# Block-sparse attention and a SoLU layer: a new order of the PV matmuls, full-row mask matmuls and an earlier fill of V's ones, in a kernel whose order of work is planned at build time

## The chip, the cores and the metric

The kernel runs on one core of one Trainium2 chip. The metric is the device time of one execution in microseconds. Executions come in a fast state and, some of them, in a slower one; only fast ones are compared here. Most slow executions here take 4 to 5 us longer. Profiles of three of them (pv_alone, pv_up_half, estimate) were kept: matmuls with 128 columns start 107 ns apart until 16.3 to 17.2 us and 56 ns apart later, while in the fast profile of the kernel before this change of pace comes at 4.7 us. The granted clock of the page (0.988 to 1.0 in these three) does not show it.

## The reference

Inputs are q, k, v of shape (4, 8, 768, 64), a list of three sampled key blocks for each of 24 query blocks, and the weights of a feed-forward layer.

```python
def _attn_ref(q, k, v, sampled_blocks):
    ...
    scores = scale * np.matmul(q, k.transpose(0, 1, 3, 2))
    mask = np.abs(blk_i - blk_j) <= 1                      # neighbouring blocks of 32
    mask = mask | (blk_i == 0) | (blk_j == 0) | (blk_i == n_blocks - 1) | (blk_j == n_blocks - 1)
    ...                                                    # and the sampled blocks
    scores = np.where(mask, scores, -1000000000.0)
    attn = softmax(scores)
    return np.matmul(attn, v)

def _moe_ref(x, w_in, w_out, g_ln):                        # x: (3072, 512)
    h = x @ w_in                                           # (3072, 1024)
    solu = h * softmax(h)
    ln = (solu - mean) / np.sqrt(var + 1e-06) * g_ln
    return (ln @ w_out).astype(np.float32)
```

## The kernel before

The mask is part of the score product: 24 further rows hold, on K's side, a one-hot code of the key block and, on Q's side, that query block's row of penalties. A score matmul therefore has 64 + 24 = 88 rows. For each batch, pair of heads and 256 queries there are three score steps of four matmuls, one exponential each on ScalarE, and three PV steps of eight matmuls:

```python
            def pv(o, n=n, pv0=pv0):
                acc = bank(pv0 or o)[:, 0 : 4 * (D + 1)].rearrange("p (a h d) -> p a h d", a=2, h=2)
                for m in range(4):
                    hh, jc = divmod(4 * n + m, NCH)
                    for qt in range(2):
                        nc.tensor.matmul(acc[:, qt, hh, :],
                                         exb[exs[n].slot][:, m, qt * P : (qt + 1) * P],
                                         va[i][:, 2 * pr + hh, jc, :], start=(n + m + qt == 0),
                                         stop=(n == 2 and m == 3 and qt == 1), skip_group_check=True)
```

V has a 65th column of ones, so that the softmax's sums come with the product.

The kernel describes its work as some 1,270 operations, each with an engine, an estimated time, its dependencies, the buffers that it takes from small pools, and a number `due`, its priority. A list scheduler inside the kernel walks through them at build time, and the instructions are then written out in exactly the order that it found:

```python
                    late = t > now + 0.02
                    key = (t if late else now, o.due)
                    if best is None or key < best[0]:
                        best = (key, o, max(t, now))
...
    A = [-275.62, -525.80, -272.33, -662.68, -957.45, -272.29, -386.71, -239.28, -1009.88, -78.24, -51.10,
...
    F = [-470.15, -35.44, -36.49, 309.28, 479.54, 383.62, -287.11, 438.46, 358.81, 675.40, 541.54, 632.99,
...
    Q = [-607.56, -1401.48, -624.25, -553.21, -198.33, 1231.82, 1169.17, 552.20, -1665.24, 7.66, 761.23,
```

`A`, `F` and `Q` are the priorities of the attention units, the feed-forward tiles and the preparations of Q and K. They look like what they are: numbers found by a search. The layer's gain g gets into w_out. A small matmul `gt` turns g, in one of two PSUM banks ("m") that it shares with the PV steps and the transposes; then VectorE scales the eight parts of w_out, which until then lie in buffers that batch 1's K and Q need:

```python
    gt = op("PE", 0.1, lambda o: nc.tensor.matmul(bank(o)[:, 0:KF], g8, identf[0:KF, 0:KF], start=True, stop=True),
            [g_load, idf, stage[("k", 0, 2)]], due=15, take="m")
    gc = op("DVE", 0.1, lambda o: nc.vector.tensor_copy(out=g_sb, in_=bank(gt)[:, 0:KF]), [gt], due=15,
            last_of=[gt])
...
    wo = [op("DVE", 0.39, lambda o, c=c: nc.vector.tensor_scalar(
        out=w_out_sb[:, c, :], in0=w_out_f[c], scalar1=g_sb[:, c : c + 1], scalar2=None,
        op0=ALU.mult), [w_out_load[c // 3], gc], due=26) for c in range(KF)]
```

The softmax here doesn't subtract the row's maximum and nothing guards it: scores larger than these inputs give would overflow.

## Time and profile before

| | before |
|---|---|
| median of 3 runs | 207.44 us (207.4 to 208.06) |
| profiled span | 205.7 us, granted clock 1.0 |
| TensorE busy | 197.6 us (96%) |
| ScalarE busy | 173.9 us (85%) |
| VectorE busy | 152.6 us (74%) |

In a profile's line of a group, `x576 | 85.4, 272 | 0.5` reads: 576 instructions, 85.4 us busy, 272 ns for one, 0.5 us of idle time before them. A matmul's own duration overlaps with that of the next (a PV matmul is recorded with 193 ns, while they start 31 ns apart), so costs are taken from the distance of two starts. A line of busy time by stretch has the stretch, its length, then PE (matmuls), PEld (weight loads), DVE (VectorE), ACT (ScalarE) and POOL (GpSimd), each with its number of instructions, then the granted clock, the DMA engines' share and GB/s.

### The profile page before, as it was taken

The page shows a single profiled execution, that of the slowest core. Times are in us where ns is not written, and L with a number is a line of the kernel's source. Part 1 is how long each engine was busy: PE and PEld are TensorE (multiplying, and loading weights), DVE is VectorE, ACT ScalarE, POOL GpSimd, SP SyncE. Part 2 cuts the span into 40 slices and gives each one's busy share as a digit, 9 for nine tenths or more (in the row PEclk, how much of TensorE's full clock was granted, in tenths as well). Part 3 has the DMA queues.
Part 4 walks back from the last instruction along what each step waited for, and adds up shares of the span by engine and source line. Part 5 has one row for each costly group of instructions (what it writes and reads, how often), then busy time and mean ns, then how long its engine had stood idle before and what let it go on. Part 6 is the DMA issues. An engine that isn't in the chain of part 4 may idle for free.

```text
span 205.7 us, 5857 instructions
## 1 busy us (share of the span) xinstructions
PE 197.6 (96%) x2304; PEld 143.1 (70%) x2332; DVE 152.6 (74%) x361; ACT 173.9 (85%) x215; POOL 63.7 (31%) x131
## 2 busy tenths in 40 slices
PE   7899999999999999999999999999999999999993
PEld 6599988777777778667777777776777655454442
DVE  4997889996788796864848675679887658788720
ACT  6799999999999999889999999998998928456532
POOL 5134015436542252154321244153310111224220
PEclk9999999999999999999999999999999999999999
DMA  5999999699996988489998969799642954668462
GB/s 155 353 381 367 261 309 116 194 270 265 307 191 155 301 211 135 87 300 246 180 232 202 247 178 195 156 328 245 118 104 66 133 163 57 150 141 189 133 205 102
DMA packets 71375, 41.80 MB, mean 203 GB/s; under 512 B 54316, under 2 KB 66868, under 8 KB 71348
## 3 DMA queue, kind: packets, MB, share of 16 engines
q1 hardware_dynamic: 70752, 40.38, 80.3%
q0 software_dynamic: 544, 1.05, 2.7%
q8 instruction: 18, 0.29, 0.6%
q14 instruction: 9, 0.07, 0.1%
q10 hardware_dynamic: 52, 0.00, 0.0%
HBM read 23.07 MB, written 6.29 MB: 143 GB/s over the span
## 4 chain that ended last, share of the span: by engine, by line
PE 85%; DVE 5%; ACT 4%; issue 2%; DMA 1%; POOL 1%; DVEq 0%; ACTq 0%; POOLq 0%
PE sbank L504 28%; PE mbank L636 20%; PE sbank L580 18%; PE mbank L525 14%; ACT ex L515 3%; DVE w_out_sb L402 3%; PE mbank L467 2%; DMA samp_i<-in_sampled_blocks_dram 1%; PE sbank L703 1%; DVE ot L647 1%; PE mbank L555 1%; ACT eso L589 1%; PE sbank L467 1%; DVE kb L445 1%; DVE x L539 0%
## 5 line engine op out<-in xcount | busy, mean ns | idle before, releaser
L515 ACT ACTIVATE ex<-sbank 128x1024 bf16<-128x1024 f32 x144 | 138.4, 1032 | 8.9 <-PE sbank L504 7.6
L504 PE MATMUL sbank<-qT,kT 88*128 88x256 bf16 x576 | 85.4, 272 | 0.5
L504 PEld LDWEIGHTS <-kT 88*128 88x128 bf16 x576 | 52.2, 97 | 23.0 <-issue 2.1
L580 PE MATMUL sbank<-w_in_sb,xT 128*128 128x512 bf16 x174 | 48.5, 379 | 0.7
L525 PEld LDWEIGHTS <-ex 128*128 128x128 bf16 x1152 | 45.0, 97 | 4.7 <-DVE x L539 0.2
L636 PE MATMUL mbank<-w_out_sb,eso 128*128 128x512 bf16 (+1 forms) x190 | 46.5, 370 | 1.0 <-DVE ot L647 0.5
L525 PE MATMUL mbank<-va,ex 128*128 128x65 bf16 x1152 | 47.2, 193 | 0.0
L593 DVE SCALAR_TENSOR_TENSOR eso<-sbank,eso 128x1024 bf16<-128x1024 f32 x24 | 29.3, 1220 | 12.1 <-ACT eso L589 12.1
L589 ACT ACTIVATE eso<-sbank 128x1024 bf16<-128x1024 f32 x24 | 24.8, 1035 | 12.0 <-PE sbank L580 4.6
L636 PEld LDWEIGHTS <-eso 128*128 128x128 bf16 x200 | 18.8, 98 | 15.5 <-issue 0.6
L606 DVE BATCH_NORM_STATS2 bn<-eso 128x6 f32<-128x512 bf16 x40 | 25.6, 682 | 0.2
L580 PEld LDWEIGHTS <-xT 128*128 128x128 bf16 x192 | 17.9, 98 | 10.3
L613 POOL TENSOR_SCALAR mv<-se,mv 128x1 f32<-128x1 f32 x24 | 6.9, 287 | 55.4 <-DVE mv L609 44.5
L647 DVE TENSOR_SCALAR ot<-mbank,rs 128x512 f32<-128x512 f32 (+1 forms) x19 | 13.9, 734 | 11.6 <-PE mbank L636 6.0
L536 DVE RECIPROCAL r<-mbank 128x4 f32<-128x4 f32 x48 | 8.4, 176 | 17.9 <-PE mbank L525 17.6
L539 DVE TENSOR_TENSOR x<-mbank,r 128x256 bf16<-128x256 f32 x48 | 19.9, 418 | 0.7
L486 POOL CAST va<-vst 128x768 bf16<-128x768 f32 x16 | 14.1, 881 | 17.2 <-DMA vst<-in_v_dram 17.1
L421 POOL CAST kb<-kst 128x768 bf16<-128x768 f32 x12 | 10.0, 831 | 21.3 <-DMA kst<-in_k_dram 21.2
L617 POOL TENSOR_TENSOR rs<-mv,neg_half 128x1 f32<-128x1 f32 x24 | 14.4, 602 | 6.6 <-ACT ot L650 3.5
L421 POOL CAST qb<-qst 128x768 bf16<-128x768 f32 x12 | 10.3, 861 | 13.1 <-DMA qst<-in_q_dram 8.6
L597 DVE TENSOR_SCALAR eso<-eso,mu 128x1024 bf16<-128x1024 bf16 x24 | 12.5, 523 | 0.2
L611 POOL TENSOR_TENSOR se<-se 128x1 f32<-128x1 f32 x24 | 4.9, 203 | 19.3 <-ACT eso L589 19.1
(74 smaller groups left out, 115.0 us busy)
## 6 DMA issues: line engine op xcount, KB each, us to landing
vst<-in_v_dram SPq DMA_DIRECT2D x16, 384.0 KB, 5.1
out_dram<-ot SPq DMA_DIRECT2D x23, 256.0 KB, 2.5
kst<-in_k_dram SPq DMA_DIRECT2D x15, 384.0 KB, 5.5
qst<-in_q_dram SPq DMA_DIRECT2D x15, 384.0 KB, 5.2
w_in_sb<-in_moe_w_in_dram POOLq DMA_DIRECT2D x2, 512.0 KB, 11.3
kT<-in_moe_w_out_dram SPq DMA_DIRECT2D x1, 768.0 KB
qT<-in_moe_w_out_dram SPq DMA_DIRECT2D x1, 768.0 KB, 13.0
eso<-in_moe_w_out_dram SPq DMA_DIRECT2D x1, 512.0 KB
```

What stands on the lines that cost most here:

```text
L421: nc.gpsimd.tensor_copy(out=half(cb[o.slot], 0).rearrange("p (c h d) -> p c h d", c=NCH, h=2), in_=st[ld.slot].rearrange("p h c d -> p c h ...
L504: nc.tensor.matmul(s[:, m, :], kT[i][0:DM, pr, hh, jc * P : (jc + 1) * P], qT[i][0:DM, pr, hh, t * TW : (t + 1) * TW], start=(m % 2 == 0), ...
L515: exs.append(op("ACT", act_us(1024), lambda o, so=so: nc.scalar.activation(out=exb[o.slot], in_=sbank[so.slot], func=ACT.Exp, scale=scale) ...
L525: nc.tensor.matmul(acc[:, qt, hh, :], exb[exs[n].slot][:, m, qt * P : (qt + 1) * P], va[i][:, 2 * pr + hh, jc, :], start=(n + m + qt == 0) ...
L539: nrm = op("DVE", 0.41, lambda o: nc.vector.tensor_tensor(out=xb[x_of[(b, t)].slot][:, :, 2 * pr * D : (2 * pr + 2) * D].rearrange("p a (h ...
L580: nc.tensor.matmul(h[:, f * 512 : (f + 1) * 512], xTb[xp.slot][:, a, c, :], w_in_sb[:, c, f * 512 : (f + 1) * 512], start=(c == 0), stop=( ...
L589: se = op("ACT", act_us(d_ff) + 0.22, lambda o, h0=h0: nc.scalar.activation(out=eb[o.slots["e"]], in_=pair(h0), func=ACT.Exp, accum_out=se ...
L593: so = op("DVE", 1.3, lambda o, h0=h0, se=se: nc.vector.scalar_tensor_tensor(out=sob[o.slot], in0=pair(h0), scalar=1.0, in1=eb[se.slots["e ...
L606: bn = op("DVE", 2 * 0.68, lambda o, so=so: [nc.vector.bn_stats(out=bnb[o.slot][:, f], in_=sob[so.slot][:, f * 512 : (f + 1) * 512]) for f ...
L617: rs = op("POOL", 0.55, lambda o, mv=mv: nc.gpsimd.tensor_tensor(out=rsb[o.slot], in0=mvb[mv.slot][:, 0:1], in1=neg_half, op=ALU.pow), [q2 ...
L636: nc.tensor.matmul(bank(o0 or o)[:, 0:w], sotb[st.slot][:, f, :], w_out_sb[:, f, col : col + w], start=(f == 0), stop=(f == KF - 1))
L647: nc.vector.tensor_scalar(out=otb[o.slot][:, 0:w], in0=bank(o0)[:, 0:w], scalar1=rsb[rs.slot], scalar2=None, op0=ALU.mult)
```

## The change

The intent: PV matmuls in an order that streams better; mask matmuls that use all 128 rows (zeros past the 24) and so need no change of the array's mode; V's ones by VectorE while it has nothing to do; the mask earlier at the start. Cut to its core:

```diff
+    PV_ORDER = [(3 - m, a) for a in range(2) for m in range(4)]
...
-    w0 = op("DVE", 0.1, lambda o: nc.vector.memset(warm, 0.0), due=-100)
+    w0 = op("DVE", 0.1, lambda o: nc.vector.memset(warm, 0.0), due=-2199.5)
...
-    selq = const.tile([NB, NCH, P], BF16, name="selq")
+    selq = const.tile([P, NCH, P], BF16, name="selq")
...
-    maskq = const.tile([NB, NB], BF16, name="maskq")
+    maskq = const.tile([P, NB], BF16, name="maskq")
...
+    sqz, mqz = fill(selq, 0.0, -2195.9), fill(maskq, 0.0, -2195.8)
...
+    for kr in krow:
+        plan.follow(kr, mq)
...
-        for lo, hi, due in ((0, TW, -2088), (TW, S, -2084.6))]
+        for lo, hi, due in ((0, TW, -2101), (TW, S, -2084.6))]
...
-    vones = [op("POOL", 0.3, lambda o, i=i: nc.gpsimd.memset(va[i][:, :, :, D : D + 1], 1.0), [stat],
-                due=-1900 if i == 0 else 0) for i in range(2)]
+    vones = [op("DVE", 0.15, lambda o, i=i: nc.vector.memset(va[i][:, :, :, D : D + 1], 1.0), due=-2195 + i)
+             for i in range(2)]
...                                          # w_in loaded by halves of its columns
-                            plan.follow(f, cas[0])
+                            plan.follow(f, qrow[(0, 0)])
...
-                for m in range(4):
+                for k, (m, qt) in enumerate(PV_ORDER):
                     hh, jc = divmod(4 * n + m, NCH)
-                    for qt in range(2):
...                                          # the matmul itself is the same; filler counts rounded otherwise;
                                           # the mask's estimate for the planner is 0.2, not 0.24
```

More of the change, by code (lines that the diff above doesn't have):

```diff
@@ L336 @@
             [last, io, samp_dma], due=-2089)
-    mq = op("DVE", 0.24, lambda o: nc.vector.scalar_tensor_tensor(
-        out=maskq, in0=anyeq, scalar=1.0, in1=static, op0=ALU.subtract, op1=ALU.mult), [last, stat], due=-2088)
+    mq = op("DVE", 0.2, lambda o: nc.vector.scalar_tensor_tensor(
+        out=maskq[0:NB], in0=anyeq, scalar=1.0, in1=static, op0=ALU.subtract, op1=ALU.mult), [last, stat, mqz], due=-2088)
     def selq_tr(o):
@@ L345 @@
     sqt = op("PE", NCH * 0.056, selq_tr, [ohs, mids], due=-2190, take="m")
-    sqs = op("ACT", 0.75, lambda o: nc.scalar.copy(out=flat(selq), in_=bank(sqt, BF16)[0:NB, 0:S]), [sqt],
+    sqs = op("ACT", 0.75, lambda o: nc.scalar.copy(out=flat(selq)[0:NB], in_=bank(sqt, BF16)[0:NB, 0:S]), [sqt, sqz],
              due=-2189, last_of=[sqt])
-    krow = [op("DVE", 0.36, lambda o, hh=hh: nc.vector.tensor_copy(out=kT[0][D:DM, 0, hh, :], in_=flat(selq)), [sqs],
+    krow = [op("DVE", 0.36, lambda o, hh=hh: nc.vector.tensor_copy(out=kT[0][D:DM, 0, hh, :], in_=flat(selq)[0:NB]), [sqs],
                due=(-2087.5, -2079.8)[hh]) for hh in range(2)]
+    for kr in krow:
+        plan.follow(kr, mq)
     mps = lambda o: bank(o)[0:NB]
@@ L383 @@
             .broadcast_to([P, 2, NCH, NB])), [mmm], due=-2076, last_of=[mmm]))
-    vones = [op("POOL", 0.3, lambda o, i=i: nc.gpsimd.memset(va[i][:, :, :, D : D + 1], 1.0), [stat],
-                due=-1900 if i == 0 else 0) for i in range(2)]
-    w_in_load = [op("POOL", 0.82, lambda o, c=c: nc.gpsimd.dma_start(
-        out=w_in_sb[:, c : c + 2], in_=moe_w_in.rearrange("(c p) f -> p c f", p=P)[:, c : c + 2]),
-        [stage[("k", 0, 3)]], due=-2000 + c, load=3.2) for c in (0, 2)]
+    vones = [op("DVE", 0.15, lambda o, i=i: nc.vector.memset(va[i][:, :, :, D : D + 1], 1.0), due=-2195 + i)
+             for i in range(2)]
+    w_in_load = [op("POOL", 0.82, lambda o, f=f: nc.gpsimd.dma_start(
+        out=w_in_sb[:, :, f : f + 512], in_=moe_w_in.rearrange("(c p) f -> p c f", p=P)[:, :, f : f + 512]),
+        [stage[("k", 0, 3)]], due=-2000 + f / 512, load=3.2) for f in range(0, d_ff, 512)]
     w_out_load = []
@@ L521, in pv @@
                 acc = bank(pv0 or o)[:, 0 : 4 * (D + 1)].rearrange("p (a h d) -> p a h d", a=2, h=2)
-                for m in range(4):
+                for k, (m, qt) in enumerate(PV_ORDER):
                     hh, jc = divmod(4 * n + m, NCH)
-                    for qt in range(2):
-                        nc.tensor.matmul(acc[:, qt, hh, :],
-                                         exb[exs[n].slot][:, m, qt * P : (qt + 1) * P],
-                                         va[i][:, 2 * pr + hh, jc, :], start=(n + m + qt == 0),
-                                         stop=(n == 2 and m == 3 and qt == 1), skip_group_check=True)
+                    nc.tensor.matmul(acc[:, qt, hh, :], exb[exs[n].slot][:, m, qt * P : (qt + 1) * P],
+                                     va[i][:, 2 * pr + hh, jc, :], start=(n + k == 0),
+                                     stop=(n == 2 and k == 7), skip_group_check=True)
             pvo = op("PE", 8 * 0.0293, pv, exs + [vc], due=A + 2.2 + 0.9 * n, take=None if n else "m",
@@ L582, in hmm @@
                                          start=(c == 0), stop=(c == KD - 1))
-                h = op("PE", 2 * 0.2156, hmm, [xp] + w_in_load, due=F[a] + 0.8 * n,
+                h = op("PE", 2 * 0.2156, hmm, [xp, w_in_load[n // 2]], due=F[a] + 0.8 * n,
                        take=None if n else ("sh" if late else "h"), last_of=[xp] if n == 3 else [],
@@ L701 @@
             if o.eng == "PE" and o.start <= begin:
-                for _ in range(max(0, int((o.start - idle) * SPARE / (0.107 if o.start < COLD else 0.0535)))):
+                gap = o.start - idle
+                for _ in range(max(0, int((gap - 0.1) / 0.107 + 0.5) if o.start < COLD else int(gap * SPARE / 0.0535))):
                     nc.tensor.matmul(flat(sbank[2])[:, 0:P], onesf, onesf, start=True, stop=True)
```

## The prediction

> **What bounds the kernel now.** I read the slice table first, then the chain that ended last, then busy time by stretch, and last the start times of single matmuls. From the page, the slices and the chain's shares:
>
> ```profile
> PE   7899999999999999999999999999999999999993
> ACT  6799999999999999889999999998998928456532
> ...
> PE 85%; DVE 5%; ACT 4%; issue 2%; DMA 1%; POOL 1%; DVEq 0%; ACTq 0%; POOLq 0%
> PE sbank L504 28%; PE mbank L636 20%; PE sbank L580 18%; PE mbank L525 14%; ACT ex L515 3%; DVE w_out_sb L402 3%; PE mbank L467 2%; DMA samp_i<-in_sampled_blocks_dram 1%; PE sbank L703 1%; DVE ot L647 1%; PE mbank L555 1%; ACT eso L589 1%; PE sbank L467 1%; DVE kb L445 1%; DVE x L539 0%
> ```
>
> TensorE is never at rest from the second slice to the last but one, and 85% of the chain that ends last lies on it. The PV steps (L525, which the change reorders) are 14% of the chain. ScalarE's row shows how near the second bound is: nine tenths until slice 32. By stretch (columns: time, then busy time of PE, PEld, DVE, ACT, POOL):
>
> ```profile
> 20.00:40.00 20.00, 19.44 (x303) 17.08 (x302) 17.76 (x38) 18.97 (x21) 5.73 (x6) 1.00 0.92 223
> 60.00:80.00 20.00, 19.79 (x276) 15.28 (x279) 16.50 (x41) 19.35 (x24) 7.83 (x14) 1.00 0.91 218
> 140.00:160.00 20.00, 19.79 (x226) 14.14 (x228) 16.23 (x38) 18.18 (x24) 5.00 (x12) 1.00 0.54 133
> 160.00:180.00 20.00, 19.84 (x165) 11.41 (x166) 14.95 (x32) 12.86 (x19) 4.19 (x12) 1.00 0.65 123
> ```
>
> So TensorE has some 1% of rest, ScalarE 3 to 9% before 160 us and much after. What TensorE saves after 40 us is worth its time until ScalarE's 3 to 9% is used up. Busy time alone would mislead, so I take the chain in order of time (columns: start, us, what), where the engine's time is not counted twice:
>
> ```profile
> 69.81 0.43 PE sbank L580 x2
> 70.24 0.74 PE mbank L525 x24
> 70.99 0.88 PE sbank L504 x8
> 71.86 0.43 PE mbank L636 x2
> 72.30 0.75 PE mbank L525 x24
> ```
>
> Back to back, one 512-wide matmul costs 0.43/2 = 215 ns, one 256-wide score 0.88/8 = 110 ns, one 65-wide PV matmul 0.75/24 = 31.2 ns. There are 144 PV steps of 8, thus 1152 matmuls and 1152 x 31.3 ns = 36.0 us of TensorE's time.
>
> **What the Trainium skill says.** (1) "Perfetto Trace Analysis", Identifying the Most-Contended Engine: matmul busy time is no measure of distance to the roofline, because matmuls overlap. This trace agrees: the page gives one PV matmul 193 ns, while they start 31 ns apart; I use start distances. (2) "TensorE: Matmul & The Clock Gate", Back-to-back issue gap: a warm, isolated matmul takes N/2.4 + 2.5 ns. The 512 and 256 widths agree (216 and 109 ns against 215 and 110). For 65 columns it gives 29.6 ns; the trace has 31.3, so 1.7 to 2.2 ns a matmul are something else. The same section's higher figures for streams with weight loads do not hold here. (3) "TensorEngine Tiling (Array Packing)", Key Properties: a change of tiling mode drains the engine. The trace agrees, below. (4) "VectorE: DVE Perf Modes", Zero memsets can be issued as uint32: one cycle an element, and a bf16 zero counts half its elements. The trace shows the identity's zero fill as 128x64 uint32 in 0.11 us.
>
> **The change part by part.**
>
> *PV order.* Before, each step takes chunk m for both query halves, then m+1. The start records, taken one by one, show a strict pattern: 515 of the 1083 distances between neighbouring PV matmuls are 29 or 30 ns, 568 are 32 to 39, and the long one almost always follows the first matmul of a pair (half 0) and the short one the second (for instance, places 2, 4, 6 of 24: 32.9, 33.6, 33.0 ns mean; places 3, 5, 7: 29.2, 29.1, 29.2). A pair therefore costs 62.5 ns, not 58.5. 29.2 ns is the stream's own floor, so the surplus is 31.35 - 29.2 = 2.15 ns x 1083 = **2.3 us**. What brings it on: each long distance follows a matmul that has just moved to the next V chunk, lying directly above the one before, and to a PSUM region below the one before. The first matmul of a step that comes after a 512-wide one moves to a new chunk too, but not from its neighbour, and mostly has 29 ns. I choose the reading that the step up to the adjoining chunk, or the move back in PSUM, costs 4 ns. The new order never steps up to an adjoining chunk within a step (3, 2, 1, 0, then back to 3) and changes PSUM region once or thrice in 8, not 7 times. Expected: about 29.3 ns a matmul, 0.235 us a step against 0.25, TensorE's total down 2.3 us.
>
> How much reaches the end: some 0.5 us of the surplus lies before 43 us, where batch 0 runs between ScalarE (8 exponentials without a break from 8.32 us) and VectorE's scaling of w_out (from 28.47 us); I count a third of it, 0.15. Of the 1.8 us after that I count four fifths, 1.5, since ScalarE is within 3 to 9% and the order on each engine is fixed. Sum: **1.6 us**.
>
> *Mask matmuls over all rows.* Matmuls only (columns: start, us):
>
> ```profile
> 8.52 0.22 PE L467 MATMUL mbank<-ident,qb 128*64 128x128 bf16 x1
> 8.67 0.28 PE L703 MATMUL sbank<-onesf 128*128 128x128 bf16 x2
> 8.79 0.60 PE L504 MATMUL sbank<-qT,kT 88*128 88x256 bf16 x4
> 9.32 0.31 PE L371 MATMUL mbank<-maskq,selq 24*128 24x24 bf16 x6
> 9.56 0.29 PE L703 MATMUL sbank<-onesf 128*128 128x128 bf16 x2
> ```
>
> Four scores from 8.79 stream for 0.44 us, to 9.23; the mask begins at 9.32, 0.09 late. Its six matmuls at 25 ns stream to 9.48; the next begins at 9.56, 0.08 late. The same gap stands ahead of 8.67 (8.52 + 0.056 = 8.58), where 64 columns change to 128. With 128 rows and 128 columns both drains of L371 go: 0.17 us of TensorE at 9.3 us. But filler matmuls (L703) stand on both sides there and ScalarE sets the pace, so I count 0. The two of L353 keep their 24 columns and so their drains.
>
> *Start.* VectorE (columns as before):
>
> ```profile
> 1.28 0.06 DVE L271 MEMSET warm<- 1x1 f32 x1
> 2.93 0.50 DVE L334 SCALAR_TENSOR_TENSOR anyeq<-kbi,samp_i,anyeq 24x24 f32<-24x24 int32 x2 [1.59 <-POOL static L317]
> 3.36 0.83 DVE L445 CAST kb<-kst 128x384 bf16<-128x384 f32 x1
> 4.36 0.35 DVE L350 COPY kT<-selq 24x768 bf16<-24x768 bf16 x1
> 4.74 0.17 DVE L337 SCALAR_TENSOR_TENSOR maskq<-anyeq,static 24x24 bf16<-24x24 f32 x1
> ```
>
> Added ahead: zeros of selq, 384 uint32 elements, 0.11 + 320/960 = 0.44 us (estimate from the row above and the skill's cycle an element); of maskq 0.06; V's ones 2 x 0.1. Together 0.7 us, ending near 2.05, inside the 1.59 us of rest before 2.93: hidden. GpSimd loses two memsets of 0.53 us and waited for data at 8.30 anyway: 0. The earlier warm memset does nothing if ScalarE's table load at 1.76 stays behind its own DMA issues. What can pay is the new rule that the copies L350 come after maskq: maskq 0.38 us earlier, the mask matmul L353 at 4.9 instead of 5.22, and ScalarE's mask copy before its three fillings of kb (L377, 1.09 us from 4.27). The first score at 6.13 waits for ScalarE's last copy at 6.07; with it gone, for VectorE's kT copy at 5.88. Gain 0.2 us, of which VectorE's unbroken row from 5.33 to 8.34 gives back some: **0.15**.
>
> *w_in by column halves, filler counts.* First used near 36 us, landing some 11 us after its issue at 15.4: 0. The fillers' rounding can add a matmul or two of 107 ns early: plus 0.05.
>
> Sum: 207.44 - 1.6 - 0.15 + 0.05 = 205.7; since the planner's model already has 29.3 ns a PV matmul and its order should fit the chip a little better, I say **205.6**.
>
> **Rivals.** (a) *Every new V chunk costs the 4 ns.* For: the short distance is always at the repeated chunk. Against: first matmuls after a 512-wide one have 29 ns with a new chunk. Then all eight of a step pay, TensorE gains 2.3 us of work and the kernel takes 208.7 to 209.5. (b) *Accumulating four times in a row into one region waits for the sum before it.* No such neighbours 29 ns apart exist in this trace, so it cannot be excluded; 207 to 210. (c) *ScalarE takes over.* For: 19.35 of 20 us. Against: ScalarE has 173.9 us in all and rests from 160 us on. The gain would shrink to 0.7 us: 206.7. (d) *The planner reshuffles.* It schedules everything anew from the changed beginning under priorities fitted to the old one; a pattern change can move 0.7 us either way. (e) *All of it passes*, with 0.6 us from the start: 204.3.
>
> **Range and chances.** I give 0.7 to my reading of the order (205.0 to 206.2 with the reshuffle), 0.2 to no or half a gain (206.3 to 207.5), 0.1 to a loss. Faster by over 2% needs 203.3, that is 4.1 us, more than PV's whole surplus plus the start: 0.05. Slower by over 2% (211.6) needs more than rival (a) and a bad reshuffle: 0.02. Range 204.3 to 207.3.
>
> **What will show it.** Right: in the chain in order of time 24 PV matmuls take 0.70 us; no alternation in the start distances; L371 128*128 without its two 0.08 us gaps; L353 and the first score 0.2 us earlier; ScalarE busier in 60 to 80 us. Wrong: 24 in 0.75 or 0.80 (rivals a, b); 0.70 with waits of scores or PV on ScalarE (c); the same sums with another order of groups (d).

## More of the kernel before

One more line is needed for the comparison, of the tile w_out_sb (shortest, middle and longest duration in ns, then first and last start in us):

```profile
L402 DVE TENSOR_SCALAR w_out_sb<-kT,g_sb x3: 480/480/486, 28.5 to 29.3; 128x512 bf16<-128x512 f32 x3
```

The scaling of w_out begins at 28.5 us.

## The result, and the profile after

| | before | changed |
|---|---|---|
| median of fast runs | 207.44 us (3 runs; a fourth, slow, took 211.36) | 229.7 us (4 runs, 228.97 to 230.01) |
| profiled span | 205.7 us | 227.3 us |
| TensorE busy | 197.6 us (96%) | 204.3 us (90%) |
| ScalarE busy | 173.9 us | 174.5 us |
| VectorE busy | 152.6 us | 154.1 us |

The changed kernel is slower by a tenth: ratio 1.1058, interval 1.1015 to 1.11. (A ratio is the mean time of one kernel's fast runs over that of the other's of the same rounds, so not quite the ratio of the medians quoted.) The work is the same but for a few short fills; TensorE rests 23.0 us in place of 8.1. Its busy time is 6.7 us longer too: 27 more filler matmuls are recorded, some 1.5 us (an estimate, at 56 ns each); the remainder was not traced further. The page of the changed kernel, slices and chain:

```profile
PE   8999999899877898887989998988799999999962
ACT  5899979977616599999999999978459967516452
...
PE 57%; ACT 17%; DVE 13%; DMA 8%; issue 3%; ACTq 0%
PE sbank L510 15%; PE sbank L584 14%; PE mbank L640 14%; ACT ex L521 13%; PE mbank L530 9%; DMA xT<-x 5%; DVE eso L597 4%; ACT eso L593 3%; PE sbank L708 2%; DMA eso<-eso 2%; DVE w_out_sb L408 2%; PE mbank L473 2%; DMA out_dram<-ot 1%; PE mbank L559 1%; DVE kT L437 1%
```

TensorE held 85% of the chain and now holds 57%; ScalarE, VectorE and DMA have taken the rest. ScalarE's row has a hole at slices 11 to 14 (6, 1, 6, 5), then a stretch of nines, then two more holes. Busy time by stretch of the changed kernel:

```profile
20.00:40.00 20.00, 19.95 (x346) 18.39 (x344) 11.41 (x29) 18.36 (x20) 4.95 (x6) 1.00 1.07 246
60.00:80.00 20.00, 15.69 (x124) 8.95 (x126) 17.50 (x42) 9.54 (x13) 4.96 (x12) 1.00 0.57 116
80.00:100.00 20.00, 17.39 (x259) 14.06 (x259) 6.44 (x20) 19.81 (x22) 4.15 (x5) 1.00 0.71 156
160.00:180.00 20.00, 18.87 (x189) 12.33 (x193) 16.40 (x37) 13.52 (x18) 4.81 (x12) 1.00 0.65 137
```

This is the picture of the loss. Attention loads ScalarE, the feed-forward layer loads VectorE, and the kernel before mixed them so that from 20 to 160 us ScalarE was busy for 18.2 to 19.4 us of each 20. Now 60 to 80 us holds almost only feed-forward work: ScalarE 9.5 us, VectorE 17.5, and TensorE, waiting for both and for transposes, 15.7. Then 80 to 100 us holds almost only attention: ScalarE full at 19.8, VectorE 6.4, TensorE 17.4. Neither stretch has much to fill its gaps with. In the chain in order of time, both kinds of wait and a PV group read

```profile
57.04 0.73 PE mbank L530 x24
...
69.50 4.60 DMA eso<-eso
74.14 1.90 PE mbank L640 x8
...
76.52 2.87 ACT ex L521 x3
```

The 4.6 us of a transpose by DMA is what the chain waits for; it is not all rest for TensorE, which between 69.5 and 74.1 us runs 16 other matmuls and rests for 0.43 and 1.25 us. Where it starts to go wrong can be seen earlier, in w_out_sb:

```profile
L408 DVE TENSOR_SCALAR w_out_sb<-kT,g_sb x3: 481/486/996, 36.8 to 38.4; 128x512 bf16<-128x512 f32 x3
```

The scaling begins at 36.8 us in place of 28.5, and VectorE has rested before it (11.4 us busy of 20, against 17.8). It ends at 44.2 us, together with the first feed-forward tile on VectorE (44.1 us).

### The profile page after: what moved, and what is told of

Read it like the earlier page. It is cut to its first block, busy times and chain, and to the rows that moved or that the text cites. A ratio compares the mean times of both kernels' runs of the same rounds, so it can differ in the third digit from the quotient of the medians.

```text
span 227.3 us, 5903 instructions
## 1 busy us (share of the span) xinstructions
PE 204.3 (90%) x2333; PEld 144.8 (64%) x2359; DVE 154.1 (68%) x365; ACT 174.5 (77%) x215; POOL 64.4 (28%) x129
## 4 chain that ended last, share of the span: by engine, by line
PE 57%; ACT 17%; DVE 13%; DMA 8%; issue 3%; ACTq 0%
PE sbank L510 15%; PE sbank L584 14%; PE mbank L640 14%; ACT ex L521 13%; PE mbank L530 9%; DMA xT<-x 5%; DVE eso L597 4%; ACT eso L593 3%; PE sbank L708 2%; DMA eso<-eso 2%; DVE w_out_sb L408 2%; PE mbank L473 2%; DMA out_dram<-ot 1%; PE mbank L559 1%; DVE kT L437 1%
## 5 line engine op out<-in xcount | busy, mean ns | idle before, releaser
L510 PE MATMUL sbank<-qT,kT 88*128 88x256 bf16 x576 | 84.2, 272 | 7.5 <-ACT ex L521 6.5
L584 PE MATMUL sbank<-w_in_sb,xT 128*128 128x512 bf16 x177 | 46.7, 379 | 5.5 <-DVE eso L597 4.2
L640 PE MATMUL mbank<-w_out_sb,eso 128*128 128x512 bf16 (+1 forms) x189 | 45.3, 370 | 3.2 <-DMA eso<-eso 1.3
L530 PEld LDWEIGHTS <-ex 128*128 128x128 bf16 x1152 | 43.7, 98 | 4.7 <-issue 0.7
L593 ACT ACTIVATE eso<-sbank 128x1024 bf16<-128x1024 f32 x24 | 24.7, 1030 | 28.4 <-PE sbank L584 22.7
L530 PE MATMUL mbank<-va,ex 128*128 128x65 bf16 x1152 | 45.6, 194 | 0.5 <-DVE ot L651 0.5
L597 DVE SCALAR_TENSOR_TENSOR eso<-sbank,eso 128x1024 bf16<-128x1024 f32 x24 | 29.3, 1221 | 14.5 <-ACT eso L593 14.2
L617 POOL TENSOR_SCALAR mv<-se,mv 128x1 f32<-128x1 f32 x24 | 7.7, 322 | 61.4 <-DVE mv L613 52.2
L601 DVE TENSOR_SCALAR eso<-eso,mu 128x1024 bf16<-128x1024 bf16 x24 | 13.0, 541 | 0.2
L708 PE MATMUL sbank<-onesf 128*128 128x128 bf16 x95 | 9.5, 239 | 1.1 <-DVE warm L273 1.1
```

The source lines that it names most:

```text
L510: nc.tensor.matmul(s[:, m, :], kT[i][0:DM, pr, hh, jc * P : (jc + 1) * P], qT[i][0:DM, pr, hh, t * TW : (t + 1) * TW], start=(m % 2 == 0), ...
L530: nc.tensor.matmul(acc[:, qt, hh, :], exb[exs[n].slot][:, m, qt * P : (qt + 1) * P], va[i][:, 2 * pr + hh, jc, :], start=(n + k == 0), sto ...
L584: nc.tensor.matmul(h[:, f * 512 : (f + 1) * 512], xTb[xp.slot][:, a, c, :], w_in_sb[:, c, f * 512 : (f + 1) * 512], start=(c == 0), stop=( ...
L593: se = op("ACT", act_us(d_ff) + 0.22, lambda o, h0=h0: nc.scalar.activation(out=eb[o.slots["e"]], in_=pair(h0), func=ACT.Exp, accum_out=se ...
L597: so = op("DVE", 1.3, lambda o, h0=h0, se=se: nc.vector.scalar_tensor_tensor(out=sob[o.slot], in0=pair(h0), scalar=1.0, in1=eb[se.slots["e ...
L640: nc.tensor.matmul(bank(o0 or o)[:, 0:w], sotb[st.slot][:, f, :], w_out_sb[:, f, col : col + w], start=(f == 0), stop=(f == KF - 1))
```

## The experiments

**Theory O (order).** The loss is the order that the planner finds. The changed beginning moves some early operations by about 0.1 us, the greedy search takes another turn somewhere, and the priorities, fitted to the old order, lead into a worse one. What speaks for it: when the kernel's own planner is run, its list ends at 198.8 for the kernel before and at 221.2 for the changed one, 22.4 later, where the chip has 22 us. (These ends are the planner's arithmetic, not times; the chip ran 8.6 and 8.5 us longer.) **Theory I (instructions).** The new instructions are to blame: sums into the same PSUM region four times running, full rows, the fills.

Going through the parts that the planner sees, one at a time, in the planner alone and not on the chip, gives an odd table: of the eight, three alone make the list end late (the rule for the copies of the one-hot rows 221.7, the rule for the fillings of kb 215.4, V's ones 221.2), and yet the whole change without the rule for the copies, or without the new place of the warm-up memset, ends at 198.8. That is no sum of costs; it fits a greedy search that decides by a threshold of 0.02 us.

### rule_only: one ordering rule, no new instruction

```diff
+    for kr in krow:
+        plan.follow(kr, mq)
```

> The kernel before with one ordering rule of the change alone (the copies of the one-hot rows come after the mask); every instruction is one of before's, of the same size. Theory O (the loss is the order in which the kernel's own planner places the work): the planner's list ends 22.9 us later than before's, so about 230 us, with TensorE idle and the scaling of w_out late, as in the changed kernel. Theory I (the loss lies in the new instructions: PV order, full-row mask, memsets): none of them is here, so 207 to 208 us.

Measured: 228.43 us, ratio 1.0977 (1.0909 to 1.1045). Every operation is one of before's (only the fillers, which follow the order, are more: 104 against 68), and the loss is there without any new instruction. The planner places TensorE's operations as in the changed kernel but for 8 of 505. The scaling of w_out begins at 36.4 us here, too, and the clump is the same:

```profile
60.00:80.00 20.00, 16.53 (x131) 9.28 (x130) 17.47 (x42) 10.54 (x14) 4.54 (x12) 1.00 0.52 115
```

### warm_back: the change with a 60 ns memset put back

```diff
-    w0 = op("DVE", 0.1, lambda o: nc.vector.memset(warm, 0.0), due=-2199.5)
+    w0 = op("DVE", 0.1, lambda o: nc.vector.memset(warm, 0.0), due=-100)
```

> The changed kernel with the one-element warm-up memset back at its old place in the list; all else as changed. Theory O: the planner's list then ends where before's does and TensorE's order after 12 us is before's, so 206 to 207 us (PV's 0.8 ns a matmul is about 0.9 us better). Theory I: 229 to 230 us, as changed, since a memset of 60 ns can't matter by itself.

Measured: 207.76 us, ratio to before 0.9979 (0.9947 to 1.0012). Of TensorE's 505 operations in the planner's list, 451 stand in another place in the changed kernel than before; here 7 do, all in the first 12 us. All the new instructions are here, and the loss is not: with rule_only before it, theory I falls. The whole loss of 22 us hangs on the place of an instruction that takes 0.06 us. The profile of this run fell in a slow execution (clock 0.855), so the kernel was run once more:

> The same kernel as warm_back again, for a profile in the fast state and a closer time. 207.7 us as before; the profile should show TensorE busy at 19.5 of 20 us or more in each stretch from 20 to 180 us and ScalarE near 19 from 20 to 140, as in the kernel before, and tell where the 0.8 us against the PV order alone is lost: if in the beginning, the first exponential starts later than 6.76 us.

Measured: 207.67 us, ratio 1.0009 (0.998 to 1.0039). The mix is back:

```profile
60.00:80.00 20.00, 19.78 (x277) 15.26 (x279) 16.32 (x42) 19.47 (x24) 8.01 (x14) 1.00 0.87 214
80.00:100.00 20.00, 19.78 (x226) 14.17 (x229) 13.37 (x33) 18.80 (x24) 7.26 (x13) 1.00 0.87 194
```

### pv_alone: the new PV order alone

The edit is the part of the diff above on PV_ORDER. The planner does not see it.

> The kernel before with the new PV order alone; the planner doesn't see it, so all orders are before's. Theory O: 24 PV matmuls take 0.73 us in place of 0.75, 206.3 to 207.0 us. Theory I in the form that summing four times in a row into one region stalls: slower than 209 us.

Measured: 207.02 us, its fast runs 206.73 to 207.11; ratio 0.9941 (0.9908 to 0.9975). The new order of PV is a small gain, no loss.

### g_own_bank: the change, with the turn of g freed from the shared banks

```diff
-    gt = op("PE", 0.1, lambda o: nc.tensor.matmul(bank(o)[:, 0:KF], g8, identf[0:KF, 0:KF], start=True, stop=True),
-            [g_load, idf, stage[("k", 0, 2)]], due=15, take="m")
+    gbank = lambda: sbank[2].rearrange("p a b -> p (a b)")[:, 512 : 512 + KF]
+    gt = op("PE", 0.1, lambda o: nc.tensor.matmul(gbank(), g8, identf[0:KF, 0:KF], start=True, stop=True),
+            [g_load, idf, stage[("k", 0, 2)]], due=15)
```

> The changed kernel, where the small matmul that turns g takes a free part of a third PSUM bank and waits for none of the two shared ones. Theory O with the late scaling of w_out as first link: scaling begins near 28 us in place of 36.8, the planner's list ends 12 us earlier, so about 217 to 218 us. If the late scaling is a mere symptom of the reshuffle: 227 to 230 us.

Measured: 216.53 us, ratio 1.04 (1.0371 to 1.0428). The tile w_out_sb:

```profile
L408 DVE TENSOR_SCALAR w_out_sb<-kT,g_sb x3: 472/477/486, 28.4 to 29.9; 128x512 bf16<-128x512 f32 x3
```

With g turned in time the scaling is back at 28.4 us, and 13 of the 22 us are gone. My reading from the code is that the late scaling is the larger link: `gt` waits for a shared bank behind work of lower `due`, w_out keeps its buffers, and batch 1's K and Q for the last two pairs cannot be copied into them. That is argued, not shown. The edit makes the planner place everything anew (428 of TensorE's 505 operations stand elsewhere than in the changed kernel), so the 13 us may come from the other order as well. And the buffers don't hold the copies up all the time: in the changed kernel the scaling ends at 44.2 us, while the first copy of K that follows it starts at 65.65 us (in g_own_bank at 47.99, before at 45.87). For the other 9 us no link was found.

### fill_only and estimate: other ways to leave the order

```diff
-                            plan.follow(f, cas[0])
+                            plan.follow(f, qrow[(0, 0)])
```

> The kernel before with another single rule of the change alone (the fillings of kb come after the first mask copy). The planner's list then ends at 215.4, against 198.8 before and 221.2 changed, and both of those ran 8.5 to 8.6 us longer on the chip. Theory O: about 224 us. Theory I: 207 to 208 us.

Measured: fast runs 220.15 to 220.83, ratio 1.0625 (1.0584 to 1.0665). Scaling of w_out begins at 28.5 us here: it is a bad order of another kind, and a scaling in time is no guard against it. The planner's list had the sign and rough size right and was 4 us off.

```diff
-            pvo = op("PE", 8 * 0.0293, pv, exs + [vc], ...
+            pvo = op("PE", 8 * 0.0295, pv, exs + [vc], ...
```

> The kernel before, with the planner told 29.5 ns a PV matmul in place of 29.3 (the chip takes 31.3); no instruction, rule or priority is changed. The planner's list ends at 211.7. Theory O in its wider form (the priorities were fitted to one order, and any small change can leave it): about 220 us. If only the changed beginning can upset it: 207 to 208 us.

Measured: fast runs 223.51 and 220.75, ratio 1.0705 (1.0614 to 1.0797); two of four runs were slow ones. Nothing in this kernel differs from before but one estimate, by 0.2 ns a matmul. The planner is told 0.2 ns more, which is nearer to the truth, and the kernel loses about 15 us. So the changed beginning isn't special: other small changes can leave the old order too, though not every one does (warm_back keeps it).

### changed_refit: the change as it is, with priorities searched anew

Only the numbers in `A`, `F` and `Q` differ from the changed kernel: 40 minutes of random steps, kept when the list ends earlier.

> The changed kernel, every instruction and rule of it, with its three lists of priorities searched anew (40 minutes of random steps, kept when the planner's list ends earlier); the list now ends at 200.9 in place of 221.2. Theory O: about 209 us. Theory I, or an order that the planner misjudges on the chip: above 215 us.

Measured: 209.36 us, ratio 1.0093 (1.0062 to 1.0124). 20 of the 22 us come back with no operation changed. By stretch:

```profile
60.00:80.00 20.00, 19.50 (x268) 15.02 (x270) 14.53 (x36) 19.66 (x24) 4.81 (x9) 1.00 0.75 168
```

### pv_down_pairs and pv_up_half: what makes a PV matmul slow

Two more orders on the kernel before, to learn why the gain was a third of the predicted:

```diff
+    PV_ORDER = [(3 - m, a) for m in range(4) for a in range(2)]     # pv_down_pairs
+    PV_ORDER = [(m, a) for a in range(2) for m in range(4)]         # pv_up_half
```

> The kernel before, PV steps with the key chunks going down but both query halves at each chunk. Theory V (a matmul whose moving V chunk lies above the one before it costs some 4 to 5 ns more; the same or a lower one costs nothing): one move up in 8, about 29.8 ns a matmul, 24 in 0.715 us, 205.8 to 206.6 us. Theory P (a change of the PSUM region costs it): seven changes in 8 as before, 31.3 ns, 24 in 0.75 us, 207.5 us.

> The kernel before, PV steps by query half with the key chunks going up. Theory V: six or seven moves up in 8, about 33 ns a matmul, 24 in 0.79 us, 208.5 to 209.5 us. Theory P: two changes of region in 8, 30.5 ns, 24 in 0.73 us, about 206.8 us.

Mean distance between neighbouring PV matmuls, from the start records, and time:

| order | ns | fast runs, us | ratio to before |
|---|---|---|---|
| chunks up, both halves at each (before) | 31.35 | 206.9 to 208.61 (both sets of rounds) | |
| chunks down, by half (the change; pv_alone) | 30.57; 30.55 | 206.73 to 207.11 (pv_alone) | 0.9941 (0.9908 to 0.9975) |
| chunks down, both halves at each | 30.61 | 206.43 to 207.12 | 0.9966 (0.9934 to 0.9998) |
| chunks up, by half | 32.22 | 208.19, 208.36 | 1.0038 (0.9992 to 1.0084) |

(The profiles of pv_alone and pv_up_half fell in slow executions; their first PV matmul starts at 18.8 and 18.3 us, after TensorE's change of pace. Those of before, changed and pv_down_pairs are fast.) In time only the two orders that go down are clear of no change. Going down is better than going up, by either grouping, and up by half is the worst: the sign of theory V. But it put 29.8 ns on pv_down_pairs, and theory P 31.3; 30.6 is neither. In that order 302 of the 1083 distances are 32 ns or more, spread over seven of the eight places of a step with no plain rule. What makes them is open.

### pv_rows and pv_refit: candidates to beat both

The kernel before with the PV order and the full rows; and the PV order with priorities searched anew from the old ones.

> The kernel before with the PV order and the mask matmuls over all rows (with their two zero fills), nothing else; the planner's list is before's. If the full rows only remove the two waits of 0.08 us at 9.3 us beside fillers: as with the PV order alone, 206.7 to 207.1 us. If the zero fills delay the beginning: 207.3 us or more.

> The kernel before with the PV order alone and priorities searched anew from before's; the planner's list ends 0.37 us earlier than before's. If the chip follows the planner: 206.3 to 206.7 us, better than both kernels. The planner's error between kernels was up to 4 us (fill_only), so 206 to 209 us would not surprise.

pv_rows: 206.68 us; ratio 0.9964 (0.9932 to 0.9995). One thing beside: in these rounds the kernel before was slow in 8 of 12 executions and pv_refit in 4 of 6, while pv_rows, changed_refit and warm_back_2, all with the full rows, were slow in none of 17. Whether the full rows do that was not tested. Its mask matmuls:

```profile
8.47 0.60 PE L508 MATMUL sbank<-qT,kT 88*128 88x256 bf16 x4
8.91 0.30 PE L375 MATMUL mbank<-maskq,selq 128*128 128x24 bf16 x6
9.06 0.27 PE L705 MATMUL sbank<-onesf 128*128 128x128 bf16 x2
```

Four scores stream for 0.44 us, to 8.91, where the mask begins at once; its six take 0.15 us, and the next begins at 9.06: both gaps of 0.08 to 0.09 us are gone, and the time is that of the PV order alone, as far as runs of different rounds tell. pv_refit: fast runs 207.12 and 206.98, ratio 0.998 (0.9934 to 1.0025): 0.4 us in the planner's list bought nothing on the chip. pv_rows has the lowest median, with both of its parts from the change, but its gain of 0.4% is clear of zero by little, and the intervals of pv_alone, pv_down_pairs and pv_rows overlap: none of the three is shown to be the best.

## Why the prediction was wrong, point by point

- **What bounds the kernel before: right, and too short.** TensorE is the bound there, because the order lets it be. I read TensorE's 1% of rest as a property of the load; it was a property of one fitted order.
- **The step that failed: rival (d), "a pattern change can move 0.7 us either way".** The mechanism was named, that the planner "schedules everything anew from the changed beginning under priorities fitted to the old one", but its size was set without a source. It measured 22 us: rule_only has the loss without any new instruction, warm_back has it removed by the place of one memset, changed_refit removes 20 of 22 us by numbers alone. In the sum itself the same error stands as "the order on each engine is fixed": 451 of TensorE's 505 operations changed places.
- **PV order: right in sign, a third in size.** Predicted 29.3 ns a matmul and 2.3 us of TensorE; measured 30.57 ns, thus 0.78 ns x 1,152 = 0.9 us, and 24 in 0.73 us against the 0.70 that I named. The long distances did not vanish but moved; the reading that a step up to the adjoining chunk is what costs explains the sign of the four orders, and the size of none of the three new ones.
- **Full rows: right.** Both drains are gone in pv_rows, and no gain in time is seen from it.
- **Start: wrong in sign.** I expected the first score 0.2 us earlier. First exponentials, before and then changed and warm_back_2:

```profile
6.76 1.02 ACT L515 ACTIVATE ex<-sbank 128x1024 bf16<-128x1024 f32 x1 [0.69 <-PE sbank L504]
```

```profile
7.43 1.02 ACT L521 ACTIVATE ex<-sbank 128x1024 bf16<-128x1024 f32 x1 [0.41 <-PE sbank L510]
```

```profile
8.21 1.02 ACT L521 ACTIVATE ex<-sbank 128x1024 bf16<-128x1024 f32 x1 [1.06 <-PE sbank L510]
```

  The fills were hidden and maskq did come earlier (3.98 us against 4.74). But the mask matmul now stands on TensorE ahead of the transposes of Q, and ScalarE's other copy has moved behind it: the first exponential is 0.7 to 1.4 us later. That this order is the cause is argued; a rival stands in the same traces. TensorE's change from 107 to 56 ns for 128 columns comes at 4.7 us before, but near 6.9 us in the changed kernel and 7.4 us in warm_back_2; in changed_refit, with the same operations, it comes by 6.1 us and the first exponential at 6.98 us. What sets this moment was not tested. warm_back lies 0.8 us above pv_alone in the same rounds, and the start is the one place where I found it behind; that this is the whole of it was not tested apart.
- **Rivals (a), (b), (c):** (a) and (b) do not hold, since pv_alone is faster than before. (c), ScalarE as the bound, did appear, from 80 to 130 us, as a result of the clumped order and not of a faster TensorE.

## What to carry to other kernels

When a kernel's order comes from a planner with fitted numbers, the numbers belong to the change: look at how much of the order a change moves before weighing its instructions, and fit the numbers again before judging it. Test the parts of such a change with the order held still, because here the parts did not add up: one rule alone cost 21 us, and the whole change with one memset put back cost nothing. An engine that is busy for 96% of the time says that the order is good, not that it will stay so; what was lost here was the mix of two kinds of work that load different engines.

## What the Trainium skill lacked or had wrong

- "TensorE: Matmul & The Clock Gate", Back-to-back issue gap: N/2.4 + 2.5 ns gives 29.6 ns for 65 columns. 29 ns does occur, but a stream means 30.55 to 32.22 ns depending on nothing but the order in which chunks and halves are taken. No page has this dependence, and the runs do not settle its rule.
- "TensorEngine Tiling (Array Packing)", Key Properties, says that a change of mode drains the engine, without a size: 0.08 to 0.09 us each way at the mask matmuls with 24 rows, and zero with 128 (pv_rows).
- No page has a cost for changing between 88 and 128 rows: in the kernel before, the first distance after such a change is 4 to 5 ns longer (112 against 108 ns for scores, 60 against 56 for transposes, 220 against 216 for the 512-wide ones, and 34 or 35 against 29 or 30 for the first PV matmul after a score).
- "TensorE: Matmul & The Clock Gate", the part on the clock gate, says that one or two busy cores do not trip the peak-current limit. One execution of a one-core program here had a mean granted clock of 0.855 and took 229.84 us against 207.7; what else ran on that die is not recorded. (The more usual slow executions, near 211.4 us, are another thing.)
